# Sinks in fp32, operands turned by TensorE, scale products a step later, and twelve unread products per step in the first attention

## The chip, the cores and the metric

The kernel runs on one core of a Trainium2 chip. TensorE (PE in the profile) multiplies, VectorE (DVE), ScalarE (ACT) and GpSimd (POOL) work element by element, SyncE (SP) and ScalarE issue transfers. Each engine takes its own instructions strictly in the order in which the program gives them and waits on semaphores for the others. The metric is the device time of one execution in microseconds.

## The reference

Three stages follow one another: attention with sinks and a sliding window, a mixture of eight experts that all tokens pass, and a cosine layer.

```python
batch, n_heads, seq, head_dim = (2, 8, 768, 64); n_sink, window = (4, 128)
keep = is_sink | in_window                     # first 4 keys, or the last 128
a = exp(where(keep, q @ k.T / 8, -1e9) - max); a = a / (a.sum(-1) + 1e-9); attn = a @ v
x = attn as (1536, 512)
P = exp(x @ w_gate - max); 8 times: rows and columns of P normalised
out = sum over e of P[:, e:e+1] * (relu(x @ w1[e]) @ w2[e])        # 512 -> 1024 -> 512
h = out @ w_in; y = (h * cos(h)) @ w_out                            # 512 -> 2048 -> 512
```

## The kernel before

Products that matter for accuracy are made from two fp16 halves: an operand is scaled, copied to fp16 (`hi`), and what is left is a second fp16 tensor (`lo`); `split` does it, the copy on ScalarE and the subtraction on VectorE or GpSimd one step later.

**First attention.** There are 48 units: two batches (b), four pairs of heads (p), six tiles of 128 queries (i). `units` lists them, 24 for each batch. The work of unit k is put into numbered steps by `put(t0, every, steps)`: `scores(k)` at step 2k (two fp32 products per unit, into banks 0 to 3), `top(k)` a step later (VectorE adds the mask, takes the maximum and makes `nm`), `expo` two steps on (ScalarE), `high`, `low` (fp16 halves, ScalarE and GpSimd), `turn` (one DMA transpose of nine 128 x 128 blocks by SyncE, five for the first tile), `values` at step 2k+13 (TensorE) and, after each group of two or three units, `norm` a step later. Batch 1 starts at step 52. `run(n)` first calls `flush()`, which issues what the step before left in `late`, then the steps put at n.

The four sink keys stand beside the window. In `low` VectorE copies their probabilities to block 0 of the unit's fp16 tile (L582) and the rest beside it (L584); the DMA transpose turns block 0 with the others, and `values` begins with two products of 130 columns against `vs` (L601), which `sinks(p)` made (L477, L478).

`prep_v` scales the values; `scales` makes a power of two from maxima: VectorE writes a diagonal (L142), TensorE multiplies it by ones (L149, `product`), VectorE reads the result (L154). `x_operand` makes the expert's seven operand blocks for a tile from the attention's output: three sums (L204 to L206), three splits (L183, L184), and a DMA transpose of fourteen blocks (L212). For batch 0 this happens six times in steps 37 to 66, VectorE taking the sums of the last three.

**Experts.** `experts` then runs layers in ticks: first products of 384 columns (L967, six per tick), then of 512 columns (L1035). Expert 0 on batch 0 shares its ticks with the remaining steps of batch 1's attention; from the operands of batch 1 on, the experts and the cosine layer have TensorE to themselves. Weights are split in the ticks of the layer before, with one call of `scales` for each.

Of the kernel before, what the change touches and what calls it, by code (L numbers as in the profile page):

```python
# [40 lines left out]
def kernel(  # L41
# [80 lines left out]
    def scales(parts, n, clamp, keep, tag, then, squares=False):  # L122
# [41 lines left out]
        late.append(product)  # L164
# [28 lines left out]
    def x_operand(b, c, i, s, place=None, g=nc.gpsimd, gl=nc.gpsimd):  # L193

        a = ACC[b]

        x = a.rearrange("p (h t) (k w) -> p h t k w", h=2, w=128)[:, :, i, c::2]
        if place is None:
# [7 lines left out]
        g.tensor_tensor(out=T[:, 0], in0=x[:, 0, 1], in1=T[:, 2], op=ALU.subtract)  # L206
        split(xs[:, 0:2, 0], xs[:, 0:2, 1], x[:, 0], s)
# [97 lines left out]
    def attention():  # L305

        banks(s=(0, 1, 2, 3), x=(4, 5), l=(6, 7))
# [26 lines left out]
        a16s, ats = Ring(parts16[:, n] for n in range(3)), Ring(parts16[:, n] for n in range(3, 7))  # L334
        more = W2S[0].rearrange("p a b w -> p (a b w)")[:, 3 * 1792:3 * 1792 + 18 * 128].rearrange("p (n a w) -> p n a w", a=9, w=128)
# [4 lines left out]
        for b, home in ((0, HH), (1, W2S[1])):  # L340
            h = home.rearrange("p a b w -> p (a b w)")
            n, n2 = 2 * NP * NT * 2 * DV, 2 * NP * 2 * DV
            vh[b] = h[:, 0:n].rearrange("p (l a t g d) -> p l a t g d", l=2, a=NP, t=NT, g=2)
            vs[b] = h[:, n:n + n2].rearrange("p (l a g d) -> p l a g d", l=2, a=NP, g=2)
# [4 lines left out]
        xss = Ring(W2S[0].rearrange("p a b w -> p (a b w)")[:, 1792 * m:1792 * (m + 1)].rearrange(  # L349
            "p (a l w) -> p a l w", l=2, w=128) for m in range(3))  # L350
# [68 lines left out]
        rep = res.tile([128, 128], F16, name="rep")  # L419
        bm = res.tile([128, 2], F32, name="bm")  # L420
        b2 = res.tile([128, 2], F32, name="bm2")

        def sink_consts():
            for t in a16s.parts:
                nc.gpsimd.memset(t[:, 0, :], 0.0)
            nc.gpsimd.memset(rep, 0.0)
            r = rep[:, 0:4 * NS].rearrange("p (g s) -> p g s", s=NS)
            nc.gpsimd.memset(r, 1.0)
            sel(r, [(0, 1, [[0, 4], [-1, NS]]), (0, -1, [[0, 4], [1, NS]])], 0.0)
            for g, t in enumerate((bm, b2)):  # L430
                nc.gpsimd.memset(t, 1.0)
                o = 2 * g * NS
                sel(t, [(-o, 1, [[-NS, 2]]), (o + NS - 1, -1, [[NS, 2]])], 0.0)
            nc.gpsimd.tensor_tensor(out=bm, in0=bm, in1=b2, op=ALU.add)
# [5 lines left out]
        def prep_v(b, groups):  # L440
# [33 lines left out]
            def sinks(p):  # L474
                ps = ring["l"].next()[:, 0:4 * DV].rearrange("p (l g d) -> p l g d", l=2, g=2)
                for hl in range(2):
                    nc.tensor.matmul(ps[:, hl], rep, vh[b][:, hl, p, 0], start=True, stop=True)  # L477
                nc.vector.tensor_tensor(  # L478
                    out=vs[b][:, :, p], in0=ps, in1=bm[:, None, :, None].to_broadcast([128, 2, 2, DV]), op=ALU.mult)
# [5 lines left out]
            for n, g in enumerate(groups):  # L485
# [5 lines left out]
                for p in range(g.start, g.stop):  # L491
                    steps.append(lambda p=p: sp(p))
                    steps.append(lambda p=p: sinks(p))
            return steps + [ones_col]
# [27 lines left out]
        S_, A_, N_, a16_, at_, X_ = {}, {}, {}, {}, {}, {}  # L522
# [35 lines left out]
        def expo(k):  # L558
# [3 lines left out]
            for ab in range(2):  # L562
                nc.scalar.activation(
                    out=Af[:, ab, 0:L], in_=Af[:, ab, 0:L], func=AF.Exp, scale=0.125,
                    bias=nm[:, ab:ab + 1])

# [9 lines left out]
        def low(k):  # L576
# [3 lines left out]
            sk = a16_[k][:, 0, 0:4 * NS].rearrange("p (g h s) -> p g h s", g=2, h=2)  # L580
            asn = A.rearrange("p h b w -> p h (b w)")[:, :, 128:TW]
            nc.vector.tensor_copy(out=sk[:, 0], in_=asn)  # L582
            between.append(
                lambda: nc.vector.tensor_tensor(out=sk[:, 1], in0=asn, in1=sk[:, 0], op=ALU.subtract))  # L584

        def turn(k):
# [3 lines left out]
                out=at[:, 0:n], in_=a16_.pop(k)[:, 0:n].rearrange("p a w -> p (a w)"))  # L590

        def values(k):
# [3 lines left out]
            if u == 0:  # L596
                X_[b] = ring["x"].next()[:, 0:n * 2 * DV].rearrange("p (u g d) -> p u g d", u=n, g=2)
            xp = X_[b][:, u]
            nb = 2 if i else 1
            for vi in range(2):  # L600
                nc.tensor.matmul(  # L601
                    xp, at[:, 0, :], vs[b][:, vi, p], start=(vi == 0), stop=False)
            for h in range(2):
                for j in range(nb):
                    for ai, vi in ((0, 0), (0, 1), (1, 0)):
                        nc.tensor.matmul(
                            xp[:, h], at[:, 1 + 2 * nb * ai + h * nb + j, :], vh[b][:, vi, p, i - (nb - 1) + j, h],
                            start=False, stop=(h == 1 and j == nb - 1 and ai == 1))
# [79 lines left out]
        def ops(b, c, i, s0):  # L688
            box = []
            put(s0, 1, [lambda: box.append(x_operand(  # L690
                b, c, i, None, *(() if b else ((Ts, xss), *((nc.gpsimd, nc.vector)[n] for n in ((0, 0), (1, 0))[c])))))])
# [16 lines left out]
        put(7, 0.5, wl1[:4])  # L708
        p0 = prep_v(0, (slice(0, 1), slice(1, NP)))
# [4 lines left out]
        put(4, 1, p0[-1:])  # L714
        put(8, 1, p0[3:4])
        put(6, 1.0, p0[4:7])
        put(10, 2, p0[7:9])
        put(12, 0.5, p0[9:-1:2])
        put(15, 2.5, p0[10:-1:2])
        put(26, 1, [prep_gate])  # L720
        put(12, 1.5, wl1[4:])
        put(28, 2.75, w1_split(0, st, range(1)))
        put(14, 2.0, [lambda p=p: load_v(1, p) for p in range(NP)])
        p1 = prep_v(1, (slice(0, NP),))
        put(24, 2.5, p1[-1:] + p1[:-1])

        def run(n):
            flush()
# [73 lines left out]
    def experts(before):  # L802
# [238 lines left out]
        def layers(e, b, act, so):  # L1041
# [24 lines left out]
            if e == E - 1:  # L1066
# [4 lines left out]
                if b:  # L1071

                    put(HT_ + 4, 7.0, xops[:3])
                    put(HT_ + GT + 9, 4.0, xops[3:])
                else:
                    put(HT_ + 4, 7.0, xops)
# [37 lines left out]
        def w2_first():  # L1114
# [24 lines left out]
            put(3.5 * NJ + 3 - 2, 1, [scl])  # L1139
# [17 lines left out]
        put(T0 + 15, 1, [lambda: put(10, 1, [probabilities()])])  # L1157
        for n, f in enumerate(sinkhorn()):
# [3 lines left out]
        for e in range(E + 2):  # L1162
# [6 lines left out]
            if e + 1 < E + 2:  # L1169
# [8 lines left out]
                if e == 1:  # L1178
                    t2, t1 = (GT + 1, GT + 10, 2, GT + 20, 1.2), (GT + 31, GT + 47, 2, GT + HT_ + GT + 4, 1.3)
# [41 lines left out]
    with tc.manual_schedule():  # L1221
        nc.gpsimd.memset(ones, 1.0)
        nc.gpsimd.memset(one16, 1.0)
        nc.gpsimd.memset(eye, 1.0)
        for cm in (1, -1):
            nc.gpsimd.affine_select(
                out=eye, in_=eye, pattern=[[-cm, 128]], compare_op=ALU.is_ge, fill=0.0, base=0,
                channel_multiplier=cm)
        experts(attention())
# [31 lines left out]
```

## Time and profile before

| | before |
|---|---|
| median of 3 runs | 1355.76 us (1353.64 to 1356.95) |
| the profiled execution | 1356.48 us, span 1354.8 us |
| PE / DVE / ACT / POOL busy | 94% / 66% / 51% / 47% |
| mean granted TensorE clock | 0.972 |

The span runs from the first to the last instruction; the time has about 1.7 us more. A busy share is an average over the whole span. The granted clock is given as a part of 2.4 GHz, so 0.50 stands for a stretch at 1.2 GHz.

### The profile page before, as it was taken

What the parts mean: (1) busy time and instruction counts of PE and PEld (TensorE: products, weight loads), DVE (VectorE), ACT (ScalarE), POOL (GpSimd) and SP (SyncE); (2) the same over time, 40 slices, a digit from 0 to 9 for tenths busy, and PEclk for the clock granted to TensorE, in tenths of its full rate; (3) what the DMA queues carried; (4) which work ended last, traced back from release to release, by engine and by line L of the source; (5) the groups of instructions that cost most, each with busy time, mean ns of one, the idle gap of its engine ahead of it and who ended that gap; (6) DMA issues with size and microseconds to landing.
All of it is one profiled execution on the core that took longest, in us unless ns stands there. A gap on an engine that the chain in (4) does not pass through costs nothing.

```text
span 1354.8 us, 19792 instructions
## 1 busy us (share of the span) xinstructions
PE 1272.4 (94%) x7299; PEld 679.7 (50%) x7299; DVE 894.3 (66%) x1852; ACT 692.4 (51%) x1382; POOL 641.1 (47%) x782
## 2 busy tenths in 40 slices
PE   5666899999999999999999999999999998999998
PEld 3543455454545545455554545555454544545554
DVE  8996852665557753854765485476557589787674
ACT  5665754463636355263534616344461748666452
POOL 4555564522435363253436426342640747377543
PEclk8768899999999999999999999999999998999999
DMA  9888653011111401501231060123102332400001
GB/s 237 172 156 196 148 119 104 1 63 63 63 62 55 148 28 36 187 16 62 76 127 59 12 194 1 62 79 124 62 17 94 55 91 41 103 1 0 32 17 47
DMA packets 140689, 108.78 MB, mean 80 GB/s; under 512 B 100144, under 2 KB 115504, under 8 KB 140592
## 3 DMA queue, kind: packets, MB, share of 16 engines
q1 hardware_dynamic: 126512, 77.22, 22.1%
q0 software_dynamic: 7168, 25.17, 6.1%
q10 hardware_dynamic: 6912, 5.13, 1.4%
q8 instruction: 57, 0.93, 0.3%
q14 instruction: 40, 0.33, 0.1%
HBM read 71.84 MB, written 11.53 MB: 62 GB/s over the span
## 4 chain that ended last, share of the span: by engine, by line
PE 70%; DVE 5%; POOL 5%; issue 3%; ACT 3%; DMA 0%; POOLq 0%; DVEq 0%
PE bank L1035 38%; PE bank L967 28%; PE bank L984 4%; DVE tmp L998 1%; POOL hh L884 1%; POOL S L275 1%; DVE w1o L190 1%; DVE tmp L904 1%; POOL S L274 1%; POOL S L276 1%; DVE tmp L895 1%; ACT tmp L900 1%; POOL S L273 0%; ACT tmp L901 0%; POOL hh L908 0%
## 5 line engine op out<-in xcount | busy, mean ns | idle before, releaser
L1035 PE MATMUL bank<-w2s,hh 128*128 128x512 f16 x2880 | 637.6, 380 | 3.0 <-POOL hh L884 2.2
L967 PE MATMUL bank<-xo,w1o 128*128 128x384 f16 x2688 | 451.1, 328 | 11.8 <-ACT tmp L935 5.2
L1035 PEld LDWEIGHTS <-hh 128*128 128x128 f16 x2880 | 281.1, 98 | 337.7 <-POOL hh L908 4.8
L884 POOL TENSOR_TENSOR hh<-tmp,hh 128x384 f16<-128x384 f32 x256 | 233.0, 929 | 368.7 <-ACT tmp L883 358.7
L967 PEld LDWEIGHTS <-w1o 128*128 128x128 f16 x2688 | 260.8, 98 | 189.2 <-issue 19.6
L935 ACT ACTIVATE tmp<-bank 128x384 f32<-128x384 f32 x192 | 93.4, 487 | 339.8 <-PE bank L967 338.7
L939 DVE TENSOR_TENSOR tmp<-bank,tmp 128x384 f32<-128x384 f32 x192 | 103.7, 553 | 178.7 <-ACT tmp L935 129.3
L984 PE MATMUL bank<-xo,w1o 128*128 128x384 f16 x672 | 119.4, 328 | 4.9 <-ACT tmp L1006 3.8
L1104 DVE SCALAR_TENSOR_TENSOR acc<-bank,PS,acc 128x512 f32<-128x512 f32 x84 | 62.9, 748 | 82.7 <-PE bank L1035 82.3
L882 ACT ACTIVATE hh<-tmp 128x384 f16<-128x384 f32 x192 | 98.9, 515 | 13.2 <-DVE tmp L939 13.2
L883 ACT ACTIVATE tmp<-tmp 128x384 f32<-128x384 f32 x192 | 100.4, 523 | 6.1
L984 PEld LDWEIGHTS <-w1o 128*128 128x128 f16 x672 | 65.7, 98 | 55.7 <-issue 8.2
L906 POOL TENSOR_SCALAR hh<-tmp 128x384 f16<-128x384 f32 x64 | 45.9, 717 | 84.0 <-DVE tmp L904 84.0
L189 ACT ACTIVATE w1o<-S,s 128x1024 f16<-128x1024 f32 x40 | 45.8, 1146 | 76.5 <-POOL S L276 75.8
L167 DVE TENSOR_REDUCE wm<-st 128x1 f32<-128x1024 f32 x68 | 81.5, 1208 | 0.0
L190 DVE SCALAR_TENSOR_TENSOR w1o<-st,s,w1o 128x512 f16<-128x512 f32 x72 | 64.9, 934 | 15.2 <-ACT w1o L189 15.2
L908 POOL TENSOR_TENSOR hh<-tmp,hh 128x384 f16<-128x384 f32 x64 | 67.8, 1059 | 5.3
L190 DVE SCALAR_TENSOR_TENSOR w1o<-S,s,w1o 128x1024 f16<-128x1024 f32 x40 | 55.2, 1380 | 20.4 <-ACT w1o L189 20.4
L998 DVE TENSOR_TENSOR tmp<-bank,tmp 128x384 f32<-128x384 f32 x112 | 59.2, 547 | 12.7 <-ACT tmp L1006 6.4
L190 DVE SCALAR_TENSOR_TENSOR w2s<-st,s,w2s 128x512 f16<-128x512 f32 x72 | 56.4, 797 | 10.3 <-ACT w2s L189 10.1
L189 ACT ACTIVATE w2s<-st,s 128x512 f16<-128x512 f32 x72 | 46.6, 708 | 22.5 <-DVE s L160 22.5
L579 POOL TENSOR_TENSOR parts<-xo,parts 128x512 f16<-128x512 f32 (+1 forms) x38 | 41.0, 1081 | 34.3 <-ACT parts L574 32.0
(187 smaller groups left out, 1313.1 us busy)
## 6 DMA issues: line engine op xcount, KB each, us to landing
st<-in_moe_w_dram SPq DMA_DIRECT2D x56, 512.0 KB, 6.1
f<-in_moe_w_in_dram POOLq DMA_DIRECT2D x16, 512.0 KB, 4.4
f<-in_moe_w_out_dram POOLq DMA_DIRECT2D x16, 512.0 KB, 4.3
w2p<-in_moe_w_dram SPq DMA_DIRECT2D x8, 512.0 KB, 4.2
w_in<-x POOLq DMA_DIRECT2D x16, 256.0 KB, 4.5
w_out<-x POOLq DMA_DIRECT2D x16, 256.0 KB, 4.3
st<-w_out SPq DMA_DIRECT2D x8, 512.0 KB, 5.3
st<-w_in SPq DMA_DIRECT2D x8, 512.0 KB, 6.7
```

Of the source, the lines that this page charges most:

```text
L167: nc.vector.tensor_reduce(out=dst, in_=src, axis=axis, op=ALU.max, apply_absolute_value=True)
L189: nc.scalar.activation(out=hi, in_=src, func=AF.Copy, scale=s)
L190: late.append(lambda: nc.vector.scalar_tensor_tensor(out=lo, in0=src, scalar=s, in1=hi, op0=ALU.mult, op1=ALU.subtract))
L882: nc.scalar.activation(out=hi, in_=src, func=AF.Relu)
L883: nc.scalar.activation(out=dst, in_=src, func=AF.Relu)
L884: nc.gpsimd.tensor_tensor(out=lo, in0=dst, in1=hi, op=ALU.subtract)
L935: nc.scalar.activation(out=t, in_=ps, func=AF.Copy)
L939: nc.vector.tensor_tensor(out=t, in0=ps, in1=t, op=ALU.add)
L967: nc.tensor.matmul(ps, W1O[:, j0 + c, wi, o, kk, :], XO[b][:, kk, o, xi, :], start=(n == 0 and o in (0, 5, 1)), stop=(n == 5), skip_group_ ...
L984: nc.tensor.matmul(ps, W1O[:, j, wi, o, kk, :], XO[b][:, kk, o, xi, :], start=(n == 0), stop=(n == 5))
L998: nc.vector.tensor_tensor(out=t, in0=x, in1=y, op=ALU.add)
L1035: nc.tensor.matmul(ps, HH[:, hi, f, t * 128:(t + 1) * 128], w[:, wi, f, :], start=(f == order[0] and n == 0), stop=(f == order[-1] and n = ...
```

## The change

Six things change in the program.

- **Sinks.** ScalarE copies each unit's eight sink columns in fp32 to a tile for the group (new L581). After the last unit of the group TensorE turns them with one fp32 product against the identity (`sink_turn`, L604), ScalarE copies the result out of bank 5 (L608; of bank 0 for batch 1), and the group's `values` begins with one fp32 product of 390 or 260 columns for all its units (L625) in place of two fp16 products per unit. VectorE's two operations per unit are gone, and the DMA transpose of a unit has eight blocks for nine (four for five).
- **Banks.** Outputs of `values` have bank 4 alone (before 4 and 5 in turn); bank 7 is for turned operands, bank 6 for the small products.
- **Operands.** For batch 0 `x_operand` has TensorE turn the seven fp32 blocks, four and then three into bank 7 (L217, two steps apart); ScalarE and VectorE split them from there. GpSimd takes all sums. The six DMA transposes of fourteen blocks are gone. Batch 1 keeps its way.
- **Scale products.** `product` of `scales` is issued one `flush` later than before, in the whole program.
- **Unread products.** Steps 2 to 57, unless a scale is being made, begin with twelve bf16 products of 128 columns into the end of bank 6 (L760). Nobody reads them. 612 are issued.
- **Times.** The first load of expert weights moves from step 7 to 14, the values of batch 1 from 14 to 20 with their preparation, some steps of later layers by one tick.

```diff
-        late.append(product)
+        late.append(lambda: late.append(product))
...
+        if turned:
+            src = [x[:, 0, 0], x[:, 0, 1], *(T[:, n] for n in range(4)), x[:, 1, 1]]
+            def turn(o):
+                ps = ring["o"].next()
+                for n, a in enumerate(src[o]):
+                    nc.tensor.transpose(ps[:, n * 128:(n + 1) * 128], a, ones)
+                ps = ps[:, 0:128 * (o.stop - o.start)].rearrange("p (a w) -> p a w", w=128)
+                hi, lo = (XO[b][:, c, o, hl, i * 128:(i + 1) * 128] for hl in range(2))
+                split(hi, lo, ps)
+                if o.start == 0:
+                    late.append(lambda: late.append(lambda: turn(slice(4, 7))))
+            return lambda: turn(slice(0, 4))
...
-        banks(s=(0, 1, 2, 3), x=(4, 5), l=(6, 7))
+        banks(s=(0, 1, 2, 3), x=(4,), l=(6,), o=(7,))
...
+            nc.scalar.activation(
+                out=sk_[0].rearrange("p (u h s) -> p u h s", u=n, h=2)[:, u], in_=Af[:, :, 128:TW], func=AF.Copy)
...
-            nc.vector.tensor_copy(out=sk[:, 0], in_=asn)
-            between.append(
-                lambda: nc.vector.tensor_tensor(out=sk[:, 1], in0=asn, in1=sk[:, 0], op=ALU.subtract))
+        def sink_turn(k, sk, rows):
+            ps = BANK[5][0:rows, 0:128] if k < KB else BANK[0][0:rows, 384:512]
+            nc.tensor.transpose(ps, sk, ones)
+            def out():
+                sk_[k] = turns.next()[0:rows]
+                nc.scalar.activation(out=sk_[k], in_=ps, func=AF.Copy)
+            late.append(out)
...
+                nc.tensor.matmul(X_[b], sk, vs[b][0:2 * n * NS, p % 2, 0:n], start=True, stop=False)
-            for vi in range(2):
-                nc.tensor.matmul(
-                    xp, at[:, 0, :], vs[b][:, vi, p], start=(vi == 0), stop=False)
...
-        put(7, 0.5, wl1[:4])
+        put(14, 0.5, wl1[:4])
...
+            for _ in range(WARM):
+                nc.tensor.matmul(BANK[6][:, 384:512], one16, eye, start=True, stop=True)
+        WARM = 12
         def run(n):
+            if 2 <= n < ends[0] - 8 and not held:
+                warm()
             flush()
```

What this makes of the order is seen in three places. On TensorE, at the start of the second group of units, before (`hh` holds the values, `parts` the turned probabilities, `xo1` keys and queries):

```order
L533 MATMUL bank2_80<-xo1_70 128x260
L533 MATMUL bank3_81<-xo1_70 128x260
...
L601 LDWEIGHTS parts_106
L601 MATMUL bank5_83<-hh_76,parts_106 128x130
...
L606 LDWEIGHTS parts_106
L606 MATMUL bank5_83<-hh_76,parts_106 128x65
```

And the same place of the changed program (`eye` and `one16` feed the unread products; the row of bank 6 stands twelve times ahead of the scores and twelve times behind them):

```order
L760 MATMUL bank6_84<-eye_92,one16_93 128x128
...
L545 MATMUL bank2_80<-xo1_70 128x260
L545 MATMUL bank3_81<-xo1_70 128x260
...
L625 MATMUL bank4_82<-hh_76,xo1_70 128x390
L631 LDWEIGHTS parts_106
L631 MATMUL bank4_82<-hh_76,parts_106 128x65
```

The group's first product is now one of fp32 with 390 columns, and it goes to bank 4 again, which the group before used.

On VectorE, one unit in the middle of the first attention, before and then changed (ISA rows are the masked maximum and its read-out, `nm` is what the exponential waits for):

```order
L582 CAST parts_106<-xo1_70 128x8
L545 ISA xo1_70,mx_412<-bank0_78,msk_121 128x260
L545 ISA mx_412 128x1
L545 ISA xo1_70,mx_412<-bank1_79,msk_121 128x260
L545 ISA mx_412 128x1
L584 TENSOR_TENSOR parts_106<-xo1_70,parts_106 128x8
L549 TENSOR_SCALAR nm_413<-mx_412 128x2
```

```order
L557 ISA xo1_70,mx_611<-bank2_80,msk_121 128x260
L557 ISA mx_611 128x1
L557 ISA xo1_70,mx_611<-bank3_81,msk_121 128x260
L557 ISA mx_611 128x1
L561 TENSOR_SCALAR nm_612<-mx_611 128x2
```

Ahead of `nm` there stands no operation on the sinks any more.

On SyncE's queue, the end of batch 0, before and then changed (L589 and L615 turn a unit's probabilities, L212 an operand):

```order
L589 DMA_TRANSPOSE parts_106<-w2s0_72 128x9x128
L212 DMA_TRANSPOSE xo0_69<-w2s0_72 128x14x128
L589 DMA_TRANSPOSE parts_106<-w2s0_72 128x5x128
L212 DMA_TRANSPOSE xo0_69<-w2s0_72 128x14x128
L589 DMA_TRANSPOSE parts_106<-parts_106 128x9x128 x2
```

```order
L615 DMA_TRANSPOSE parts_106<-parts_106 128x8x128 x3
L615 DMA_TRANSPOSE parts_106<-w2s0_72 128x8x128
L615 DMA_TRANSPOSE parts_106<-w2s0_72 128x4x128
L615 DMA_TRANSPOSE parts_106<-parts_106 128x8x128 x3
```

The operands' transposes have left the queue; on TensorE they are the following rows, with the step's other work between the fours and the threes:

```order
L217 MATMUL bank7_85<-ones_86,acc0_74 128x128 x2
L217 MATMUL bank7_85<-ones_86,hh_76 128x128 x2
L545 MATMUL bank0_78<-xo1_70 128x260
...
L217 MATMUL bank7_85<-ones_86,hh_76 128x128 x2
L217 MATMUL bank7_85<-ones_86,acc0_74 128x128
```

## Rows read from the trace of the kernel before

**Rows 1.** Windows: length, busy us (instructions) of PE, PEld, DVE, ACT, POOL; granted clock, DMA share, GB/s.

```profile
7.00:32.00 25.00, 15.63 (x68) 11.51 (x68) 23.12 (x90) 16.50 (x35) 9.15 (x25) 0.86 1.10 266
32.00:86.00 54.00, 33.07 (x327) 26.23 (x328) 50.85 (x197) 33.89 (x75) 31.79 (x36) 0.80 0.88 166
86.00:111.00 25.00, 13.26 (x82) 7.83 (x81) 17.46 (x72) 13.33 (x30) 10.23 (x10) 0.50 0.91 190
111.00:155.00 44.00, 33.12 (x294) 18.81 (x292) 35.97 (x101) 27.67 (x57) 26.59 (x29) 0.88 0.77 179
155.00:216.00 61.00, 57.91 (x486) 31.33 (x486) 31.54 (x108) 34.70 (x73) 34.37 (x41) 0.97 0.60 116
216.00:1355.00 1139.00, 1119.30 (x6051) 583.80 (x6048) 732.04 (x1281) 565.07 (x1112) 523.76 (x613) 1.00 0.20 64
```

**Rows 2.** Windows of DVE's L582 alone: length, busy us (count), clock, DMA share, GB/s.

```profile
7.00:32.00 25.00, 1.11 (x7) 0.86 1.10 266
7.00:86.00 79.00, 8.55 (x24) 0.82 0.95 198
111.00:155.00 44.00, 4.73 (x8) 0.88 0.77 179
```

**Rows 3.** The same windows of DVE's L584 alone.

```profile
7.00:32.00 25.00, 1.90 (x6) 0.86 1.10 266
7.00:86.00 79.00, 7.15 (x24) 0.82 0.95 198
111.00:155.00 44.00, 3.75 (x9) 0.88 0.77 179
```

**Rows 4.** Groups of DVE, 7 to 111 us: busy, mean ns, idle before.

```profile
L549 DVE TENSOR_SCALAR nm<-mx 128x2 f32<-128x2 f32 x31 | 7.1, 229 | 0.1
L618 DVE TENSOR_TENSOR acc<-bank,ri 128x384 f32<-128x384 f32 x6 | 3.3, 557 | 0.2
```

**Rows 5.** Timeline at 13.5 us: start, length, engine, idle before and its releaser.

```profile
13.52 0.16 DVE L584 TENSOR_TENSOR parts<-xo,parts 128x8 f16<-128x8 f32 x1
13.55 1.15 POOL L579 TENSOR_TENSOR parts<-xo,parts 128x512 f16<-128x512 f32 x1 [2.63 <-ACT parts L574]
13.64 1.09 DVE L549 TENSOR_SCALAR nm<-mx 128x2 f32<-128x2 f32 x1
```

**Rows 6.** Timeline of PE, 47 to 53 us.

```profile
47.54 2.08 PE L533 MATMUL bank<-xo,xo 128*128 128x260 f32 x4
...
51.24 0.28 PE L601 MATMUL bank<-hh,parts 128*128 128x130 f16 x2
51.35 0.53 PE L606 MATMUL bank<-hh,parts 128*128 128x65 f16 x12
51.71 1.12 PE L533 MATMUL bank<-xo,xo 128*128 128x260 f32 x4
52.67 0.28 PE L601 MATMUL bank<-hh,parts 128*128 128x130 f16 x2
```

**Rows 7.** A piece of the chain that ended last: start, us, what.

```profile
484.03 31.08 PE bank L1035 x144
```

**Rows 8.** Waits of PE, 86 to 111 us: total, times, longest.

```profile
PE bank L967 <- DMA xo<-w2s: 4.7, 1, 4.7
PE bank L601 <- DMA parts<-parts: 3.6, 1, 3.6
```

**Rows 9.** Transfers, 176 to 216 us: the queue's packets, MB, share; an issue's us to landing.

```profile
q1 hardware_dynamic: 16888, 4.33, 58.6%
...
xo<-xs SPq DMA_TRANSPOSE x6, 4.0
```

**Rows 10.** Timeline of PE where expert 0 first needs the last operand.

```profile
110.78 1.12 PE L967 MATMUL bank<-xo,w1o 128*128 128x384 f16 x3 [4.69 <-DMA xo<-w2s]
```

**Rows 11.** A wait of PE, 111 to 155 us.

```profile
PE bank L601 <- DVE acc L618: 3.3, 2, 2.3
```

**Rows 12.** A wait of PE, 1000 to 1355 us.

```profile
PE bank L149 <- DVE diag L142: 5.4, 3, 2.5
```

More of the change, by code (lines that the diff above doesn't have):

```diff
@@ L334, in attention @@
         a16s, ats = Ring(parts16[:, n] for n in range(3)), Ring(parts16[:, n] for n in range(3, 7))
+        asks = Ring(parts16[:, n, 0].bitcast(F32) for n in range(3))
+        turns = Ring([TMP.rearrange("p a b -> p (a b)")[:, 4096 + S:4096 + S + 128], carve(128)])
         more = W2S[0].rearrange("p a b w -> p (a b w)")[:, 3 * 1792:3 * 1792 + 18 * 128].rearrange("p (n a w) -> p n a w", a=9, w=128)
@@ L415, in attention @@
                 blk(snk, [(128 * i - window, 1, -1)])
-        rep = res.tile([128, 128], F16, name="rep")
-        bm = res.tile([128, 2], F32, name="bm")
-        b2 = res.tile([128, 2], F32, name="bm2")
+        G = 2 * U3
+        rep = res.tile([128, G * NS], F16, name="rep")
+        bm = res.tile([128, G], F32, name="bm")
         def sink_consts():
[L424 to L434, printed above, removed]
+            nc.gpsimd.memset(rep, 1.0)
+            sel(rep.rearrange("p (g s) -> p g s", s=NS), [(0, 1, [[0, G], [-1, NS]]), (0, -1, [[0, G], [1, NS]])], 0.0)
+            nc.gpsimd.memset(bm, 1.0)
+            sel(bm, [(0, 1, [[-NS, G]]), (NS - 1, -1, [[NS, G]])], 0.0)
         siv, rv = {}, {}
@@ L490, in prep_v @@
                     steps.append(common)
[L491 to L494, printed above, removed]
+                steps += [lambda p=p: sp(p) for p in range(g.start, g.stop)]
+            return steps, ones_col, [lambda p=p: sinks(p) for p in range(NP)]
         swg = []
@@ L565, in expo @@
                     bias=nm[:, ab:ab + 1])
+            _, u, n = sums[k]
+            if u == 0:
+                sk_[0] = asks.next()[:, 0:2 * n * NS]
+            nc.scalar.activation(
+                out=sk_[0].rearrange("p (u h s) -> p u h s", u=n, h=2)[:, u], in_=Af[:, :, 128:TW], func=AF.Copy)
+            if u == n - 1:
+                sk = sk_[0]
+                late.append(lambda: late.append(lambda: sink_turn(k, sk, 2 * n * NS)))
         def blocks(k, hl):
@@ L589, in turn @@
             nc.sync.dma_start_transpose(
-                out=at[:, 0:n], in_=a16_.pop(k)[:, 0:n].rearrange("p a w -> p (a w)"))
+                out=at[:, 1:n], in_=a16_.pop(k)[:, 1:n].rearrange("p a w -> p (a w)"))
         def values(k):
@@ L713, in attention, with warm @@
         put(6, 1, p0[2:3])
[L714 to L725, printed above, removed]
+        put(4, 1, [c0])
+        put(8, 1, k0[:1])
+        put(6, 1.0, p0[3:6])
+        put(9, 4, p0[6:8])
+        put(13, 0.5, p0[8:])
+        put(17, 1, k0[1:2])
+        put(30, 1, [prep_gate])
+        put(20, 1.5, wl1[4:])
+        put(31, 2.75, w1_split(0, st, range(1)))
+        put(20, 2.0, [lambda p=p: load_v(1, p) for p in range(NP)])
+        p1, c1, k1 = prep_v(1, (slice(0, NP),))
+        put(27, 2.1, [c1, *p1[:5], lambda: None, *p1[5:]])
+        put(52, 7, k1[:2])
+        for p in range(2, NP):
+            put(turned[(p - 1) * NT - 1] + 1, 1, k0[p:p + 1])
+            put(turned[KB + (p - 1) * NT - 1] + 1, 1, k1[p:p + 1])
+        def warm():
+            for _ in range(WARM):
+                nc.tensor.matmul(BANK[6][:, 384:512], one16, eye, start=True, stop=True)
+        WARM = 12
         def run(n):
+            if 2 <= n < ends[0] - 8 and not held:
+                warm()
             flush()
@@ L1221 @@
     with tc.manual_schedule():
-        nc.gpsimd.memset(ones, 1.0)
         nc.gpsimd.memset(one16, 1.0)
@@ L1228 @@
                 channel_multiplier=cm)
+        nc.gpsimd.tensor_copy(out=ones, in_=eye)
         experts(attention())
```

40 lines of the change are left out of this document (21 added, 19 removed).

## Prediction

> **What bounds the kernel now.** I read the windows by stage first [rows 1]. Look for the engine that is nearly always busy. From 7 to 32 us it is VectorE (23.12 of 25 us) and from 32 to 86 us again (50.85 of 54), while TensorE works 15.63 and 33.07 us at a granted clock of 0.86 and 0.80. From 86 to 111 us nobody is full: TensorE works 13.26 of 25 us, all of it at 0.50, that is 1.2 GHz. From 111 to 155 us VectorE (35.97) and TensorE (33.12 of 44) share the bound, and from 155 us on TensorE has it (57.91 of 61, then 1119.30 of 1139 at 1.00). So 1200 of 1355 us are TensorE's own work, which the change leaves nearly as it is; what it can move lies in the first 155 us.
>
> The waits of TensorE say what ends the gap at 86 to 111 us: 4.7 us for the DMA transpose of the last operand and 3.6 us for the transposes of the turned probabilities [rows 8]; the first product of expert 0 that needs the last operand starts at 110.78 [rows 10]. These transposes share one queue and the DMA engines, whose busy share is 0.91 there [rows 1].
>
> I call the stages A (7 to 32), B (32 to 86), C (86 to 111), D (111 to 155), E (to 216) and F.
>
> **Prices.** A pair of scores takes 0.96 us where the clock is up (52.67 less 51.71) and 2.08 where it is down; the twelve value products 0.36 (51.35 to 51.71), the two products with the sinks 0.11 (51.24 to 51.35) [rows 6]. In F, 144 products of 512 columns take 31.08 us [rows 7], 0.42 ns per column. An unread product of 128 columns is then 0.054 us, a step's twelve 0.65, and twice that at the lower clock. A pair of scores is 520 fp32 columns in 0.96 us, 1.85 ns each: the new product with the sinks is 0.72 us for 390 columns and 0.48 for 260. No row shows a turn of a 128-column fp32 block. If it streams like fp16 it takes 0.054 us, if like the fp32 scores 0.24; between ends so far apart I take 0.15, since turn and scores read the same type. For the DMA transposes only a mixed row exists: the queue filled 58.6% of 16 engines over 40 us (375 engine-us) [rows 9], for 129 blocks by my count of six transposes of fourteen and five of nine. That is about 0.18 us of all engines per block, 2.5 us for an operand.
>
> **Sinks off VectorE.** In A the two operations take 1.11 + 1.90 = 3.0 us in 13 instructions [rows 2, 3]. Undisturbed, one takes 0.16 us [rows 5]; 13 of them are 2.1 us of work, and 0.9 is waiting. At 13.5 us the reader sees what for: L584 takes 0.16, GpSimd's L579 starts at 13.55 and ends at 14.70, and the next VectorE operation, `nm`, of two columns, takes 1.09 and ends at 14.73 [rows 5]; the mean of `nm` is 0.229 [rows 4]. Whichever small operation of VectorE meets GpSimd's subtraction waits. Without the sinks `nm` can meet it more often, so I keep half of the waiting: A gains 2.5 and takes 22.5. TensorE fits: 15.63 us x 0.86 is 13.4 at the full clock, and twelve steps of unread products add 7.8, 21.2 in all.
>
> The Trainium skill ("SBUF — State Buffer", section "SBUF: two separate sides") calls the port pair that VectorE and GpSimd share an exclusive lock, held for a whole instruction. The trace agrees (1.09 us for `nm`), and by that rule all waiting would pass to `nm`: A would gain 2.1 and D, below, 2.7 for 5.6, and the time would be 3 us longer than my sum.
>
> **Stage B changes its bound.** VectorE loses 15.70 - 3.01 = 12.7 us in 35 instructions; with half of the waiting kept, 9.1, which leaves 41.7 us. But TensorE now has, at the full clock: scores 14.4 (sixteen units, the short first tiles counted in part, as fifteen), values 6.1 (17 sets), the sinks' products 4.1 (five of 390 columns, one of 260), 28 operand turns 4.2, sink turns 0.8, and unread products in 32 steps 20.8: 50.4 us. Then there is one bank for the outputs. The first product of a group must wait until VectorE has read the group before, and scores and unread products are queued behind it, and VectorE waits for these scores. The wait exists in D: 3.3 us for L618 [rows 11], over about four groups 0.8 each. The read alone takes 0.557 [rows 4], the longest such wait 2.3 [rows 11]. Six groups at 0.8 are 4.8, so B takes 55.2, **1.2 more** than now. The waits for the scale's read of bank 6 lie under `held`, where no unread products are issued: nothing, bounded by a VectorE read of some 0.5.
>
> **Stage C loses its two DMA waits.** 4.7 + 3.6 = 8.3 us; the queue drops the 14-block transposes, and a unit's has eight blocks for nine. What is late next is the chain GpSimd sums, TensorE turns, ScalarE and VectorE splits; I leave 0.8 us for it, as for one wait of D. **7.5 gained.** VectorE is no new bound: 17.46 us [rows 1], with sinks and the last operand's sums still in them.
>
> **D and E.** In D VectorE drops 4.73 + 3.75 = 8.5 us in 17 instructions, 2.7 of work and 5.8 of waiting, half of it kept: 5.6. Batch 1's nine groups add to TensorE 6 x 0.72 + 3 x 0.48 + 9 x 0.15 = 7.1 and drop 24 x 0.11 = 2.6: 4.5 more, half in D (2.3) and half in E, where TensorE has no air (2.2). D gains 3.3, E loses 2.2.
>
> **F.** Three products of scales wait 5.4 us for VectorE's diagonal [rows 12]. Each moves behind the next tick's first products, six of 384 columns, 0.98 us: at most 2.9 us come back. What then waits behind the later scale is a split, which was moved a tick earlier or later with it; the weights are needed a whole layer on. 2.9 gained, and nothing if the diagonal itself comes later.
>
> **At nothing.** The weight load moved from step 7 to 14 frees the DMA engines in A (share 1.10 [rows 1]); VectorE, not a load, fills A, so I count none. The copies on ScalarE (48, and nine of the turned sinks) fall to an engine that is busy 16.50 of 25 and 33.89 of 54 us [rows 1]; they would cost where `high` waits behind them, about 0.2 us per unit, under VectorE in A and under TensorE in B.
>
> **The sum.** -2.5 + 1.2 - 7.5 - 3.3 + 2.2 - 2.9 = -12.8. The profiled execution took 1356.48 us (span 1354.8 and about 1.7 around it), 0.7 above the median of the runs; 1356.48 - 12.8 - 0.7 = **1343**.
>
> **Rivals.**
>
> *More is gained* (0.20). The turns stream like fp16 (B 2.7 less, C 1.3 less), the bank has always been read in time (4.8), and the waits behind GpSimd go with the sinks (0.5 in A, 2.9 in D). That is 12.2 more: 1331. For it: B's TensorE would still fit with 47.7 us, over VectorE's 41.7. Against it: [rows 11] show the bank's wait with two banks in turn.
>
> *Nothing is gained: the single bank* (0.17). VectorE's read stands behind tops and, before the diagonals, behind long work; if each group waits the 2.3 us that are the longest of [rows 11], B takes 50.4 + 13.8 = 64.2, 9.0 more than I say. If the new chain in C costs 2.5 more than I left, the total is -1.3: about 1354.
>
> *Slower: the unread products do not lift the clock* (0.13). This is where the change doesn't do what it says. They are then 28.6 us of work at a price that the clock sets. At 0.80, the clock of B now, A takes 21.2 / 0.80 = 26.5 and B 50.4 / 0.80 + 4.8 = 67.8, 16.6 more than I say: +3.8, 1359.5; at 0.75 1365. It decides at a mean clock in A and B of 71.6 / 85.7 = 0.84, where the whole change comes out even. Against it: TensorE would be busy 21.2 of 22.5 and 50.4 of 55.2 us, and a stretch that is busy 57.91 of 61 has 0.97; for it: 15.63 of 25 has 0.86, and 13.26 of 25 has 0.50 [rows 1].
>
> The Trainium skill ("TensorE: Matmul & The Clock Gate", Part 4) says that transposes in TensorE's own mode do not count as busy for the clock as products do; no row here shows it, and by it the 28 turns would speak for this rival.
>
> **How the numbers follow.** My forecast has 0.50, the rivals 0.20, 0.17 and 0.13. The forecast's own range is 1336 to 1350: the turn's two ends move it by 5 down and 4 up in B and C, the scales' term by 2.9. The whole range, 1329 to 1358, takes in the first two rivals, and leaves out most of the third and the far end of the first, 0.18 together. A change of 0.3%, 4 us, is about what a measurement of this kernel can tell from none. Faster: 0.48 of the forecast, 0.20, and 0.04 of the single bank's case, 0.72. Same: 0.02, 0.10 and 0.03 of the slow case, 0.15. Slower: 0.13.
>
> **What would show it.** Stage A ends with VectorE's maximum for unit 8, B with that for unit 24. In the changed profile these should come at about 29.5 us and 85 us, and expert 0's first product with the last operand at 102 (now 110.78); the clock from 7 to 85 us should be above 0.95, TensorE there busy over 85%, and VectorE under 80%. TensorE's waits should name VectorE's read of the outputs (L618 before) about six times, with 0.8 us each, and no DMA of an operand before 105 us. A turn's own length decides between 0.054 and 0.24. The clock staying under 0.84, or the bank's wait at over 2 us, would make the forecast wrong on the slow side; a B of under 50 us on the fast side.

## The result, and the profile after

The changed kernel takes 1362.42 us (median of 5 runs, 1361.45 to 1364.27), the kernel before, run beside it, 1356.39: ratio 1.0054, 95% interval 1.0043 to 1.0065. It is slower by 6 to 9 us where 12.8 less were forecast, and outside the range of 1329 to 1358. The profiled execution took 1361.45 us, span 1359.7; it is the fastest of the five, so the two traces differ by 4.9 us and not by all of the loss.

The windows of the changed kernel, same stretches and columns as [rows 1]:

```profile
7.00:32.00 25.00, 21.33 (x244) 18.18 (x245) 21.63 (x79) 15.49 (x40) 9.05 (x17) 1.00 1.01 219
32.00:86.00 54.00, 49.33 (x624) 41.47 (x624) 39.90 (x152) 38.56 (x96) 26.81 (x31) 0.97 0.81 145
86.00:111.00 25.00, 21.35 (x229) 14.42 (x228) 16.64 (x58) 14.07 (x36) 11.33 (x15) 0.88 0.55 105
111.00:155.00 44.00, 34.87 (x275) 18.67 (x273) 31.77 (x83) 29.49 (x69) 27.43 (x30) 0.87 0.82 174
155.00:216.00 61.00, 58.17 (x470) 29.69 (x469) 29.95 (x92) 37.34 (x89) 34.01 (x42) 0.97 0.51 108
216.00:1355.00 1139.00, 1123.07 (x6072) 584.76 (x6071) 733.75 (x1280) 566.01 (x1114) 526.45 (x615) 1.00 0.20 64
```

The reader sees what the change set out to do done: the granted clock from 7 to 86 us rose from 0.86 and 0.80 to 1.00 and 0.97, VectorE's busy time there fell by 12.4 us (74.0 to 61.5), DMA's share at 86 to 111 us from 0.91 to 0.55. But equal windows do not hold equal work: at 86 us the changed kernel is behind. Up to the maximum of unit 24, which comes at 86.66 us before and at 92.37 after, VectorE is busy 8.4 us less and not 12.4 (the third time is VectorE's):

```profile
7.00:86.66 79.66, 49.36 (x396) 37.78 (x396) 74.59 (x289) 50.81 (x111) 41.36 (x61) 0.81 0.95 199
7.00:92.37 85.37, 76.09 (x952) 63.92 (x953) 66.17 (x242) 56.47 (x140) 37.78 (x51) 0.98 0.86 168
```

So the time must be sought at milestones, not in busy shares. I take five from each trace: the starts of `nm` for units 8, 24, 31 and 40 (counted from 0), and ScalarE's 13th read of an expert's first products (L935 before, L974 after, near 216 us). The lengths between them, in us; the stretches are the forecast's stages A, B, then C with what follows to unit 31, and so on, so C and D, and D and E, can trade a microsecond:

| kernel | A, to unit 8 | B, to 24 | C, to 31 | D, to 40 | E, to the read | F, to the end |
|---|---|---|---|---|---|---|
| before | 32.9 | 53.8 | 27.4 | 42.6 | 59.8 | 1138.4 |
| changed | 32.1 | 60.3 | 23.5 | 44.2 | 61.8 | 1137.8 |
| difference | -0.8 | +6.5 | -3.9 | +1.6 | +2.1 | -0.6 |
| forecast | -2.5 | +1.2 | -7.5 | -3.3 | +2.2 | -2.9 |

Every stage but E came out worse than forecast, B and D most. Each length is of a single trace. e11 and e16 below are one kernel, and their D differs by 1.5; e10, whose edit starts with batch 1, has B 2.8 longer than the changed kernel. A difference of one stage below about 3 us shows little by itself.

Waits of TensorE from 7 to 86 us (total, times, longest), then two of VectorE from 86 to 116 us:

```profile
PE bank L760 <- DVE hh L490: 5.2, 4, 2.8
PE bank L625 <- DVE acc L643: 1.6, 2, 1.2
PE bank L760 <- DVE allm L154: 1.0, 1, 1.0
```

```profile
DVE xo L557 <- ACT tmp L608: 4.7, 1, 4.7
DVE xo L557 <- PE bank L545: 3.5, 3, 1.4
```

The unread products (L760) wait for VectorE's read of the value sinks (L490) in their own bank. The 4.7 us of VectorE, put down to ScalarE's copy of turned sinks (L608), are mostly a wait for the scores: these start at 113.38 us, behind an expert's products, and the copy in the same bank is itself released by them:

```profile
113.38 1.24 PE L545 MATMUL bank<-xo 64*128 64x260 f32 x4
114.64 0.27 ACT L608 ACTIVATE tmp<-bank 24x128 f32<-24x128 f32 x1 [2.02 <-PE bank L545]
115.05 0.43 DVE L557 CUSTOM_DVE_ANT_0 xo<-bank,msk 128x260 f32<-128x260 f32 x1 [4.66 <-ACT tmp L608]
```

The DMA waits of [rows 8] are gone, as forecast.

### The profile page after: what moved, and what is told of

Same layout as the page of the kernel before. It is cut to its first block, busy times and chain, and to the rows that moved or that the text cites. A ratio compares the mean times of both kernels' runs of the same rounds, so it can differ in the third digit from the quotient of the medians.

```text
span 1359.7 us, 20914 instructions
## 1 busy us (share of the span) xinstructions
PE 1309.9 (96%) x7911; PEld 708.2 (52%) x7911; DVE 877.7 (65%) x1747; ACT 702.2 (52%) x1442; POOL 640.3 (47%) x776
## 4 chain that ended last, share of the span: by engine, by line
PE 73%; DVE 9%; ACT 6%; POOL 5%; issue 5%; DMA 2%; ACTq 0%; POOLq 0%; DVEq 0%
PE bank L1074 35%; PE bank L1006 28%; PE bank L1023 4%; PE bank L545 2%; DVE tmp L1037 2%; PE bank L760 1%; DMA xo<-xs 1%; POOL hh L923 1%; PE bank L625 1%; DVE w1o L191 1%; DVE tmp L943 1%; DVE xo L557 1%; PE bank L631 1%; ACT w2s L190 1%; DVE tmp L934 1%
## 5 line engine op out<-in xcount | busy, mean ns | idle before, releaser
L1006 PEld LDWEIGHTS <-w1o 128*128 128x128 f16 x2688 | 260.6, 98 | 183.3 <-issue 12.8
L974 ACT ACTIVATE tmp<-bank 128x384 f32<-128x384 f32 x192 | 93.4, 487 | 336.4 <-PE bank L1006 335.8
L191 DVE SCALAR_TENSOR_TENSOR w1o<-st,s,w1o 128x512 f16<-128x512 f32 x72 | 65.4, 941 | 13.5 <-ACT w1o L190 13.4
```

The lines of the kernel that those rows point to most:

```text
L191: late.append(lambda: nc.vector.scalar_tensor_tensor(out=lo, in0=src, scalar=s, in1=hi, op0=ALU.mult, op1=ALU.subtract))
L974: nc.scalar.activation(out=t, in_=ps, func=AF.Copy)
L1006: nc.tensor.matmul(ps, W1O[:, j0 + c, wi, o, kk, :], XO[b][:, kk, o, xi, :], start=(n == 0 and o in (0, 5, 1)), stop=(n == 5), skip_group_ ...
```

## The experiments

Each ratio is to the kernel before run beside it, with its 95% interval; us are medians. 0.001 of the ratio is 1.36 us.

**e1 to e4: the unread products and their bank.**

```diff
-        WARM = 12
+        WARM = 0          # e1; 6 in e2
```

```diff
-  ps = (ring["l"].next() if b == 0 else BANK[1][:, 264:])[0:G * NS, 0:2 * DV]...   # e3
+  ps = BANK[5 if b == 0 else 1][:, 264:][0:G * NS, 0:2 * DV]...
```

```diff
-        banks(s=(0, 1, 2, 3), x=(4, 5), l=(6, 7))     # e4, in the kernel before
+        banks(s=(0, 1, 2, 3), x=(4, 5), l=(6,))
         def run(n):
+            if 2 <= n < 58 and not held:
+                for _ in range(12):
+                    nc.tensor.matmul(BANK[7][:, 384:512], one16, eye, start=True, stop=True)
             flush()
```

> The changed kernel without the unread products (none in place of twelve per step); all else stays. Theory W (TensorE's own work is the new bound between units 8 and 24, 2.9 us per unit, of which 1.34 are unread products): the units there come every 2.4 to 2.6 us again, but the granted clock falls back to about 0.8, so a part is given back in slower scores; about 1355, 7 us under the changed kernel. Theory V (the loss is TensorE's wait for VectorE's read of the bank of small products, which the unread products share): those 6.3 us of waits vanish too, about 1355. Theory S (sinks and turns on TensorE are what costs): stays at 1362 or gets worse, since the slower clock makes them dearer. This run tells S from the other two.

> The changed kernel with six unread products per step in place of twelve. Theory W: 0.33 us less in each step, 11 us of TensorE work in the 33 steps of that stage, of which 5 to 8 come back before VectorE binds; the clock stays over 0.9; about 1355. Theory V: the waits for the shared bank stay as they are, only their number of products changes: 1360 to 1362. If the clock needs the twelve: granted clock in 32 to 86 us back to 0.8 and no gain.

> The changed kernel, but the small products of the value sinks of batch 0 go to the free columns of bank 5 (that of the turned sinks) in place of bank 6, so that the unread products no longer wait for VectorE's read of them. Theory V: 5.3 us of waits on that read vanish, and with them the stretch of low clock behind the longest (2.8 us); 1354 to 1357. Theory W: TensorE catches up only what it idled, VectorE and the chain hold the rest; 1358 to 1361.

> The kernel before with one part of the change alone: twelve unread products at the head of each of steps 2 to 57, into bank 7, and the small products in bank 6 alone. Theory W: TensorE has about 45 us of work between units 8 and 24, still under VectorE's 51, so nothing is lost there, and the faster clock shortens the gap from 86 to 111 us by 1 to 3 us, in which two transfers are waited for: 1353 to 1356. Rival: the unread products lose time by themselves, as they stand ahead of each score that VectorE waits for: 1359 or more.

Measured: e1 1362.60, 1.0063 [1.0048, 1.0078]; e2 1365.48, 1.0083 [1.0053, 1.0112]; e3 1360.47, 1.0051 [1.0033, 1.0069]; e4 1355.41, 1.0009 [0.9999, 1.0018]. Theories W and V both fall. Without the unread products the kernel is as slow as with them; added to the kernel before they change nothing that can be told. Their clock is paid for by their work: e1 has B 4.3 shorter than the changed kernel (56.0) and C 3.7 longer (27.2), with the clock at 0.50 from 86 to 111 us where the changed kernel has 0.88. Taking the wait on their bank away (e3) moves unit 24 by 1.9 us and the time by nothing certain. e2 is a miss that I can't explain: its four runs spread over 9 us, and its profile, of the fastest, has the clock at 0.91 between 32 and 86 us. What is left by e1 is theory S, sinks and turns; the steps that the change moved stay in e1 too. The window 32 to 86 us of e1:

```profile
32.00:86.00 54.00, 38.63 (x298) 25.79 (x298) 43.02 (x153) 40.37 (x101) 28.23 (x32) 0.78 0.88 153
```

Here nobody is full, and B is still no shorter than before (2.2 longer). That speaks against a bound by one engine's sum.

**e5 to e8: each part alone.** e5 is the changed kernel with the unread products, the turned operands and the later scales undone; e6 puts `x_operand` of the change, with banks l=(6,) and o=(7,), into the kernel before; e7 is e6 with e4's unread products, in bank 6; e8:

```diff
-        late.append(product)
+        late.append(lambda: late.append(product))
-        put(10, 2, p0[7:9])
-        put(12, 0.5, p0[9:-1:2])
+        put(9, 4, p0[7:9])
+        put(13, 0.5, p0[9:-1:2])
...
```

> Of the change only the sinks on TensorE, with the banks and the times in the first attention that go with them; no unread products, the operands of batch 0 by DMA transposes with VectorE's sums, the scale products at their old place. Theory T (the sinks' part is what costs: TensorE's products and turns, the single bank for outputs, and in batch 1 scores that wait for ScalarE's copy of the turned sinks out of their bank): 5 us lost where TensorE binds, 1 to 4 more before; 1360 to 1364. Theory R (the forecast: VectorE's relief pays): 1347 to 1352.

> The kernel before with the operands of batch 0 turned by TensorE alone (bank 7 for them, bank 6 for the small products, two banks for outputs as before, all sums on GpSimd). Theory T: the wait for the last operand's transposes (4.7 us) goes and some of the 3.6 for the other transposes, 4 to 6 gained; 1349 to 1352. Theory O (the turns are what costs, 42 fp32 turns and a longer chain through ScalarE): 1357 to 1361.

> The kernel before with the turned operands and the unread products together, sinks and scale products as before. Theory T: the gap after unit 24 loses its DMA waits and runs at a faster clock, nothing is lost between units 8 and 24 since TensorE's 45 to 49 us stay under VectorE's 51; 1346 to 1350, faster than both kernels. Theory O: 1357 or more, since turns and unread products together fill TensorE there.

> The kernel before with the scale products one step later alone (and two preparation steps and the layers' steps moved with them, as in the change). By the forecast 2.9 us come back of three waits of TensorE for a diagonal in the last layers: 1352 to 1353. Rival (the wait passes to the next transfer or split in the chain): 1354 to 1356.

Measured: e5 1361.54, 1.0056 [1.0043, 1.0069]; e6 1352.07, 0.9980 [0.9971, 0.9989]; e7 1354.64, 1.0005 [0.9995, 1.0014]; e8 1353.71, 0.9997 [0.9988, 1.0005]. The sinks' part, with the banks and moved steps that go with it, loses what the whole change loses; no run has the moved steps of the loads and of batch 1's values alone. The turned operands gain 2.7 us, and unread products beside them take that back (e7 was expected to be the best, and is not). The window 32 to 86 us of e5, and a wait of TensorE from 7 to 86 us:

```profile
32.00:86.00 54.00, 38.36 (x261) 26.07 (x261) 44.15 (x155) 39.82 (x102) 30.54 (x34) 0.70 0.77 157
```

```profile
PE bank L627 <- DVE acc L645: 7.5, 4, 2.5
```

VectorE is relieved (44.15 for 50.85 of 54), yet B is 4.5 longer: TensorE waits four times, up to 2.5 us, until VectorE has read the one bank of outputs (L645 there), with the scores queued behind. e1 shows the same wait, 7.6 us in four between units 8 and 24.

e8 shows where the later scales' gain in F went. Waits of TensorE from 1000 to 1355 us in e8; before, the diagonal had 5.4 us [rows 12]:

```profile
PE bank L984 <- DMA xo<-xs: 2.7, 2, 1.4
PE bank L1035 <- POOL hh L908: 2.7, 6, 0.8
PE bank L149 <- DVE diag L142: 2.6, 2, 1.7
```

The diagonal's wait has halved, and the operands' transposes (1.0 before) and GpSimd's `hh` (0.5 before) are waited for 3.9 us longer.

**e9, e15: two output banks.** e9 from e5, e15 from e1:

```diff
-        banks(s=(0, 1, 2, 3), x=(4,), l=(6,), o=(7,))
+        banks(s=(0, 1, 2, 3), x=(4, 5), l=(6,), o=(7,))
-            ps = BANK[5][0:rows, 0:128] if k < KB else BANK[0][0:rows, 384:512]
+            if k < KB and held:
+                late.append(lambda: sink_turn(k, sk, rows))
+                return
+            ps = BANK[6][0:rows, 384:512] if k < KB else BANK[0][0:rows, 384:512]
...
```

> The kernel of e5 (sinks alone) with two banks for the outputs as before; the turned sinks of batch 0 go to the end of bank 6, a step later where a scale is being made there. Theory B (the single output bank is what makes units 8 to 24 slower): the 7.5 us in which TensorE waits there for VectorE's read of the outputs vanish, and 3 to 5 us come back, 1357 to 1359. Theory P (the loss is TensorE's own added work and the bank shared with scores in batch 1): 1360 to 1362, unit 24 still later than in the kernel before.

> The changed kernel with two banks for the outputs of the values (turned sinks of batch 0 at the end of bank 6, a step later where a scale is being made) and no unread products. Theory B (the single bank, which also holds up the operands' chain, eats the gain): 1351 to 1354, under the kernel before. Rival (sinks on TensorE cost what the operands gain, whatever the banks): 1356 to 1359.

Measured: e9 1358.74, 1.0026 [1.0016, 1.0036]; e15 1356.62, 1.0021 [1.0008, 1.0034]. Against e5 and e1 the second bank is worth 0.0030 and 0.0042, 4 and 6 us, with intervals apart: in kernels without unread products the single bank is a cause, shown; with them it has no run. Where it acts is less clear. From e5 to e9 B falls by 2.8, but from e1 to e15 it rises by 1.4, and it is C that falls by 7.1, at a clock of 0.78 from 86 to 111 us for 0.50. And the edit brings waits of its own, since the turned sinks now share bank 6 with the scale products. In e9 and then in e15, between units 8 and 24, turns wait for ScalarE's copies of the sink columns (L587, L585), and scale products for its copies out of bank 6 (L619, L617):

```profile
PE bank L615 <- ACT parts L587: 6.0, 3, 3.6
PE bank L153 <- ACT xo L619: 3.1, 1, 3.1
```

```profile
PE bank L153 <- ACT xo L617: 5.3, 2, 3.0
PE bank L613 <- ACT parts L585: 2.8, 2, 2.5
```

Both stay above the kernel before, and e15 ends inside its rival's range, at the low end. What the sinks cost with a second bank and no shared bank 6 has no run.

**e10, e13: what batch 1's sinks cost the new way and the old.** e10, in the changed kernel (e13 does the same in the kernel before):

```diff
+            if k >= KB:          # expo: no copy, no turn
+                return
...
+                if k < KB:           # values: no product with the sinks
                     sk = sk_.pop(k + n - 1)
                     nc.tensor.matmul(X_[b], sk, ...)
```

> The changed kernel with the sinks of batch 1 left out altogether (no copies, no turns, no products with them, so batch 1's outputs lack the sinks). It prices batch 1's part on TensorE and in the bank of the scores. Theory P: 5 to 8 us under the changed kernel, 1354 to 1357: from unit 31 on nothing more is lost against the kernel before. Theory B (the loss sits before, in batch 0): 1 to 3 us under it, 1359 to 1361.

> The kernel before with the sinks of batch 1 left out (VectorE's two operations per unit, the two products with them, their block of the transposes and their preparation; batch 1's outputs lack the sinks). By the forecast VectorE's two operations hold up the stage from 111 to 155 us, so 5.6 us and the 2.6 of products come back: 1347. Theory P (TensorE's work sets these stages, VectorE's operations lie beside it): only the 2.6 us of products and 0 to 2 more come back, 1351 to 1353, so that the new way, 11 us, costs some 7 to 9 us more than the old.

Measured: e10 1351.26, 0.9972 [0.9958, 0.9985]; e13 1345.59, 0.9938 [0.9925, 0.9951]. The new way costs 1.0054 - 0.9972 = 0.0082, 11 us, with the intervals 9 to 13; the old 0.0062, 8 us, 7 to 10. That the new way is dearer is thus likely and not shown. Theory P is right that the new way is dear and wrong that the old was cheap: e13 came out as the forecast's 5.6 + 2.6 said. D is 4.3 and E 2.8 shorter in e13 than before, and in e10 2.1 and 4.9 shorter than in the changed kernel: by these single traces (e10's is 4 us above its median) the swap gives a little in D and takes it in E.

**e12, e14: two single waits.**

```diff
-        put(13, 0.5, p0[8:])          # e12
+        put(13, 1.5, p0[8:])
```

```diff
-            late.append(out)          # e14, for batch 1
+            out()
```

> The changed kernel, but the three last splits of batch 0's values stand in steps 13, 14 and 16 in place of 13, 13 and 14. Theory Q (VectorE's relief is there, 5 us at unit 6, and is given back at once, since three splits now stand in one row ahead of unit 7's maximum): unit 8 comes 1 to 3 us earlier than in the changed kernel, and 0 to 2 us of that reach the end, 1360 to 1362. Rival (unit 7 waits for something else, such as scores or transfers): unit 8 stays at 32 us.

> The changed kernel, but ScalarE's copy of the turned sinks of batch 1 stands directly behind the turn, not a step later, so that the next unit's scores wait less for the bank that they share. If the shared bank is a large part of the 11 us: 2 to 4 us less than the changed kernel, 1358 to 1360, and VectorE's 4.7 us wait for that copy is gone. If it is TensorE's work: 1361 to 1363.

Measured: e12 1364.27, 1.0063 [1.0048, 1.0078]; e14 1360.65, 1.0046 [1.0029, 1.0062]. In e12 unit 8 does not come earlier (32.7), so theory Q falls as it was put; the third split only moved behind unit 7 and still stands ahead of unit 8. In e14 VectorE's wait for the copy is gone by name, but a wait for the scores has taken its place (`DVE xo L557 <- PE bank L545: 6.3, 3, 4.2` where the changed kernel has 4.7 and 3.5); C is 1.7 shorter and D 1.5 longer; the time moves within its interval.

**e11, e16: the two parts that gained, together.** e6 and e8 in one kernel; a product for value sinks that finds bank 6 held goes a step later.

> The kernel before with the two parts that gained by themselves, operands turned by TensorE and scale products a step later; sinks as before, no unread products. If the gains add, 2.5 + 0.9: 1351, 0.25% under the kernel before and under both kernels; if the later scales hide the turned operands' gain or the other way round, 1352 to 1354.

> The kernel of e11 once more, on the chip of e15: 1348 to 1352, again under both kernels by more than 0.25%.

Measured: 1349.18, 0.9955 [0.9941, 0.9970], and again 1349.83, 0.9967 [0.9955, 0.9979]: **faster than the kernel before by 4 to 6 us, and than the changed one by about 12.** By the medians that is more than e6's and e8's gains together, though not clear of their intervals; the edit to the value sinks, which neither has, has no run of its own. Windows of e11 from 32 and from 86 us, and all waits of TensorE from 86 to 111 us:

```profile
32.00:86.00 54.00, 38.35 (x363) 30.18 (x360) 49.10 (x199) 32.16 (x68) 27.76 (x33) 0.79 0.80 156
86.00:111.00 25.00, 20.45 (x140) 12.82 (x141) 18.46 (x75) 14.80 (x32) 11.91 (x16) 0.73 0.66 123
```

```profile
PE bank L553 <- DVE mx L565: 1.7, 2, 0.9
PE bank L216 <- DVE xo L184: 1.7, 3, 0.8
PE bank L216 <- POOL hh L208: 1.1, 1, 1.1
```

C is 6.1 us shorter than before and B no longer (53.5) at the old clock of B (0.79; C's is 0.73 for 0.50), with VectorE's sinks in place.

## Why the prediction was wrong

**"Stage B changes its bound" is the step that failed first**, by the sizes of its terms. B was to take 55.2 us and took 60.3; TensorE's sum, the larger of the two as forecast, is 4.4 of the 5.1 between them.

- *TensorE's sum* was 50.4 and is 54.8 of the 60.3 us between units 8 and 24. The unread products take 0.67 to 0.76 us a step (47.37 to 48.04 and 45.57 to 46.33, below) for 0.65, some 24 us in 33 steps for 20.8; the fp32 product with 390 columns takes 0.85 (46.33 to 47.18) for 0.72, while a turned block takes 0.11 for 0.15.
- *Its waits* were to be six of 0.8 us for the one bank. There are three, 2.5 us in all; but "nothing" for the unread products' wait in bank 6 is 4.6, since `held` covers scales, not the value sinks:

```profile
PE bank L760 <- DVE hh L490: 4.6, 3, 2.8
PE bank L625 <- DVE acc L643: 2.5, 3, 1.2
```

- *VectorE's relief*, 11.6 us in A and B, is 8.4 for equal work, with all else that the change moves on VectorE. The forecast added up the lengths of short operations, and in the trace these overlap their neighbours. Unit 6, whose two operations took an undisturbed 0.16 and 0.17 us, shows it, before and then changed:

```profile
28.03 0.17 DVE L582 CAST w2s<-xo 128x8 f16<-128x8 f32 x1
28.10 0.29 DVE L545 CUSTOM_DVE_ANT_0 xo<-bank,msk 128x132 f32<-128x132 f32 x1
...
28.53 0.16 DVE L584 TENSOR_TENSOR w2s<-xo,w2s 128x8 f16<-128x8 f32 x1
28.65 0.17 DVE L549 TENSOR_SCALAR nm<-mx 128x2 f32<-128x2 f32 x1
```

```profile
23.02 0.29 DVE L557 CUSTOM_DVE_ANT_0 xo<-bank,msk 128x132 f32<-128x132 f32 x1
...
23.57 0.17 DVE L561 TENSOR_SCALAR nm<-mx 128x2 f32<-128x2 f32 x1
```

From the first maximum to `nm` there are 0.55 us with L584 and 0.55 without it, and L582 holds up the maximum by 0.07. The forecast priced each at 0.16.

The clock came as forecast. In the changed kernel TensorE is thus nearly full in B. But e1 and e5 show B no shorter without any unread product, with no engine full, and with the bank's wait grown to 7.6 us and more: scores, maximum, values and the read of the one bank wait for each other in a ring. That reading is argued from the waits. Of all rivals the single bank was nearest: its 2.3 us per wait is what e5 shows (up to 2.5), though the changed kernel does not (1.2), and e9 and e15 price it at 4 to 6 us of the whole. The rest of the sinks' loss stays open, with the moved steps and the shared bank 6 as rivals.

**"A gains 2.5"** came out at 0.8, and no run shows even this to be the sinks. VectorE in the changed kernel:

```profile
24.16 0.62 DVE L188 TENSOR_SCALAR hh<-acc,sv 128x768 f16<-128x768 f32 x1
26.22 4.23 DVE L191 SCALAR_TENSOR_TENSOR hh<-acc,sv,hh 128x768 f16<-128x768 f32 x3 [1.44 <-ACT hh L190]
...
31.17 0.17 DVE L561 TENSOR_SCALAR nm<-mx 128x2 f32<-128x2 f32 x1
```

Unit 6 has its `nm` at 23.57, before at 28.65. That looks like the relief, and is not: e8, with both operations on VectorE, has it at 24.22, and unit 8 0.8 us earlier than before, as the changed kernel has. What e8 shares with the change, and the list of the change leaves out, are moved steps in the preparation of batch 0's values (before `put(10, 2, ...)` and `put(12, 0.5, ...)`, then `put(9, 4, ...)` and `put(13, 0.5, ...)`). e5, with these steps and the scale products at their old place, has unit 6 at 22.87; e6, with the old steps, at 27.14. Of three splits two stood ahead of unit 6; now all stand behind it and ahead of unit 7. Of the waiting behind GpSimd a part is passed on to `nm`. The groups of VectorE from 7 to 111 us show it; `nm` had 229 ns [rows 4]:

```profile
L561 DVE TENSOR_SCALAR nm<-mx 128x2 f32<-128x2 f32 x31 | 9.9, 320 | 1.1
```

That is 2.8 us more, where the sinks' operations had waited for about 8 up to 86 us by the forecast's price (15.7 us [rows 2, 3] less 48 of 0.16): less than the half that the forecast kept.

The Trainium skill ("SBUF — State Buffer", section "SBUF: two separate sides") has VectorE and GpSimd lock each other out of a shared port pair for whole instructions, and the trace agrees in kind: `nm` takes longer, 320 ns in the mean, but by far less than all that the sinks' operations had waited, so what the forecast drew from the lock, that all waiting would pass to `nm`, did not come.

**"7.5 gained" in C** was nearly right as a mechanism: the DMA waits went, and e11 has 6.1 of it, e15 7.3. The changed kernel keeps 3.9, and the new chain costs more than 0.8 in it: the waits of TensorE from 86 to 111 us that replace the two have 1.8 us for the turned sinks, 1.3 for the one bank and 0.7 for the splits. The forecast also left out a third wait of that window, 3.5 us of scores for VectorE's maximum (`PE bank L533 <- DVE mx L545: 3.5, 4, 1.9`). The turned sinks of batch 1 share bank 0 with scores, and the scores wait for ScalarE's copy, which stands behind the exponentials:

```profile
102.50 0.28 PE L604 MATMUL bank<-ones,parts 128*24 128x128 f32 x1
...
103.53 0.90 ACT L575 ACTIVATE xo<-xo,nm 128x260 f32<-128x260 f32 x2
...
104.58 0.25 ACT L608 ACTIVATE xo<-bank 24x128 f32<-24x128 f32 x1
...
104.88 0.60 PE L545 MATMUL bank<-xo,tmp 64*128 64x260 f32 x2 [1.77 <-ACT xo L608]
```

No price was given to that shared bank at all; in e14's trace it is worth 1.7 us in C, and D is 1.5 longer.

**"D gains 3.3"** became +1.6. Its price for VectorE's sinks was right in sum (e13), with 4.3 us of it in D for 5.6; the mis-sized term is what replaces them, 7.1 us by the forecast and 11 by e10, the waits for the banks among them. D's own sign says less: e8, e11 and e16, with the sinks on VectorE, have it 1.0, 2.0 and 3.5 longer than before. **E** came as forecast (2.1 for 2.2), in part by luck: e12, which moves three early splits and nothing else, has 3.7. **"2.9 gained" in F** was 0.6. Its own sentence looked for a split behind the later scale; by e8 it is the next transfer and GpSimd that are late there, and the wait passes to them.

The rival of the slow clock fell in its mechanism (0.97 to 1.00), though the time ended, by chance, where it said. The gains of the parts do not add: the turned operands with later scales take 4 to 6 us from the kernel before, and about nothing from the sinks' part with two banks (e9 to e15). In e15 the operands still bring C to 20.1, but B is 3.9 longer than in e11, and E, with the sinks' work on a full TensorE, 4.8. Whether that is all of it stays open.

## What to carry to other kernels

Relieving the busiest engine pays only up to the next wait: price a short operation from its start to the next one's, not by its length, and before adding up engine sums, follow one buffer around (who fills the bank, who empties it, what is queued behind each), and price a bank that is taken away as a wait on every turn. Work that moves to an engine which is full later in the program costs there what it saved here. Raising a clock with unread work was worth nothing here, where that work then stood in the queue. Compare equal work and not equal windows, and try the parts of a change alone, the moved steps too: one part lost more than two others gained, and an earlier maximum that looked like the sinks' relief came with moved steps of the preparation.

## What the runs showed of the hardware

Turning a 128 x 128 fp32 block takes TensorE about 0.11 us at the full clock (102.62 to 102.83 for two), twice the 0.056 of a bf16 product of 128 columns (47.37 to 48.04 for twelve), and the fp32 product of 24 rows and 390 columns 0.85 us, 2.2 ns per column. Unread products, a product with turned sinks and a turned operand in the changed kernel, at a granted clock of 1.00:

```profile
45.57 0.83 PE L760 MATMUL bank<-eye,one 128*128 128x128 bf16 x12 [0.64 <-DVE hh L490]
46.33 0.92 PE L625 MATMUL bank<-hh,tmp 24*128 24x390 f32 x2
47.18 0.36 PE L631 MATMUL bank<-hh,parts 128*128 128x65 f16 x6
47.37 0.83 PE L760 MATMUL bank<-eye,one 128*128 128x128 bf16 x12
48.04 1.09 PE L545 MATMUL bank<-xo,xo 128*128 128x260 f32 x4
...
102.62 0.38 PE L217 MATMUL bank<-ones,hh 128*128 128x128 f32 x2
102.83 0.27 PE L217 MATMUL bank<-ones,acc 128*128 128x128 f32 x1
```

With twelve products of 128 columns at the head of a step, and the small products in one bank for two (e4), the granted clock was 0.97 to 1.00 between 7 and 86 us, where it was 0.80 to 0.86.
